# A fused attention and two-stage MoE kernel: a shorter rolled loop for other expert pairs, and one step for each piece of the router

## The chip, the cores and the metric

The kernel runs as one program on one core of a Trainium2 chip. The time is the device time in microseconds (us) of one execution. The profile is of one further execution of the same program. TensorE is called PE, VectorE DVE, ScalarE ACT, GpSimd POOL; SP is the engine that issues most DMAs. PEld is PE's weight load, which overlaps its products.

## The reference, cut to what matters

```python
scores = scale * q @ k.T + bias           # 4 batches, 8 heads, 576 tokens, head size 64
x = (softmax(scores) @ v)                 # -> x [2304, 512], 4 batches of 576 tokens
# first MoE: 8 experts of 512 -> 1024 -> 512, one expert for each token
e_idx = argmax(x @ w_gate);  g = softmax(x @ w_gate)[e_idx];  eom = sigmoid(x @ w_output_gate)
for e in range(8):
    mask = e_idx == e
    out[mask] = g[mask] * eom[mask, e] * (relu(x[mask] @ w1[e]) @ w2[e])
# then a dense gated layer 512 -> 1536 -> 512
return (silu(x @ w_gate) * (x @ w_val)) @ w_out
```

## The kernel before

Attention comes first. The first MoE then works on pairs (batch b, expert e). For each batch the kernel computes the router, finds the first expert that the batch's tokens chose, and runs that expert densely over all 576 tokens, with the gate set to zero for tokens that chose another. Tokens that chose another expert form *other pairs*: one small pair (128 tokens or fewer) is gathered and done by the functions `q_...`; all further pairs go through `loop()`, a loop whose count T is read from the device's list at run time. With T = 0 each engine jumps over the loop's code.

The four dense pairs make 64 steps, numbered n = 16 b + s. At step n PE does `h_step` of step n+1 (12 products, x times a 128-wide slice of w1, into the PSUM tile T) and then `y_step` of step n (12 products with a slice of w2). ACT and DVE turn each h into a high and a low part (tile qz, L544 and L545). After these, step n runs the functions that a table `todo` has for it, in the order in which `at(n, f)` put them there; all engines take their instructions in that order. For batch b = 1, 2, 3 the functions start at n = 16 b - 15 (steps 1, 17, 33):

- `router(b)` has seven pieces: `logits` (PE products lps L370, ACT copies lraw L371), `logits_t` (PE transposes L379, DVE sums L382), `shift` and `gates` (small DVE operations), `gates_2` (DVE L400 to L405, the gates ex), `spread` (PE transposes the gates into gps L412 and counts tokens L415; ACT copies them out L418 to L420; SP stores the gates, L421) and `first` (eight small DVE operations L425 to L432: flags and e0i, the batch's first expert).
- `m_load(b, gi)`: SP reads e0i and loads that expert's weights (L486, L487), the first two parts at step n+7 and n+8; `m_conv` splits slice f into a high and a low half at step n+9+f (ACT and DVE, L503 and L505).
- At step 40 batch 3's `first` is followed by `ranks` of the pair list (PE transposes the flags, L447).

Batch 0's router is done before, by `moe_early`. After step 63 come `q_h` and `q_y` for the small pair (L657 to L672), with `loop()` before the last two slices, then `q_old` (loads xl, L705) and `q_out` (L681 to L700), and after that the dense gated layer (L1179 to L1201), whose weights are narrowed on DVE while its first chunk runs.

Of the kernel before, what the change touches and what calls it, by code (L numbers as in the profile page):

```python
# [9 lines left out]
F32 = mybir.dt.float32  # L10
# [4 lines left out]
ALU = mybir.AluOpType  # L15
# [6 lines left out]
NP = H // 2  # L22
# [11 lines left out]
VL = (7, 12, 13, 14)  # L34
LG = (1, 5, 5, 7, 8, 10, 10)
N0, PRE, FL, LEAD = 6, 3, 0, 0
QN = (43, 46, 44, 46, 49, 54, 56)
EL, EC = ((47, 51, 53), (50, 51, 51, 52, 55, 55))
QT, SX = (44, 2)
# [68 lines left out]
def body(tc, qt, kt, va, vb, ws, moe_w_gate, moe_w_output_gate, moe_w1, moe_w2, w_gate, w_val, w_out, ctab, cst, cst2, out):  # L108
    nc = tc.nc
    with ExitStack() as ctx:  # L110
# [4 lines left out]
        vw = att.enter_context(tc.tile_pool(name="vw", bufs=1))  # L115
# [34 lines left out]
        for r in range(4):  # L150
            o = slice(32 * r, 32 * r + 32)
# [7 lines left out]
        vt = {}  # L159
# [101 lines left out]
        def t_tile():  # L261
            return pO.tile([128, 512], F32, tag="T", bufs=2, name="T")
# [81 lines left out]
        hbuf = {}  # L344
# [135 lines left out]
        def load_w(e, gi, tag="vt"):  # L480

            n = min(3, 8 - 3 * gi)
            t = vw.tile([128, 3072], F32, tag=tag, bufs=1 if tag == "rv" else 2, name="raww")
            a = t[:, 0:512 * n].rearrange("p (k f) -> p k f", k=4)
            c = t[:, 1536:1536 + 512 * n].rearrange("p (f d) -> p f d", f=n)
            nc.sync.dma_start(a, moe_w1[bass.ds(e, 1), :, 384 * gi:384 * gi + 128 * n].rearrange("o (k p) f -> p (o k) f", p=128))  # L486
            nc.sync.dma_start(c, moe_w2[bass.ds(e, 1), 384 * gi:384 * gi + 128 * n].rearrange("o (f p) d -> p (o f) d", p=128))  # L487
            return [(a[:, :, 128 * i:128 * i + 128], c[:, i]) for i in range(n)]
# [3 lines left out]
        def conv_w(raw, f, later=None):  # L492

            a, c = raw
            if f < 4:
                ta = ap.tile([128, 2, 4, 128], F32R, tag="ph", bufs=4, name="w1hl")
                tb = ap.tile([128, 2, 4, 128], F32R, tag="bias", bufs=4, name="w2hl")
            else:
                t = ap.tile([128, 2, 2, 4, 128], F32R, tag=("pt0", "pt1")[f // 6], bufs=2, name="whl")
                ta, tb = t[:, 0], t[:, 1]  # L500
            cc = c.rearrange("p (d m) -> p d m", m=128)
            for x, y in ((a, ta), (cc, tb)):
                nc.scalar.activation(y[:, 0], x, AF.Copy)  # L503
                if later is None:
                    nc.vector.tensor_tensor(y[:, 1], x, y[:, 0].bitcast(F32), ALU.subtract)  # L505
                else:
                    later.append(lambda x=x, y=y: nc.vector.tensor_tensor(y[:, 1], x, y[:, 0].bitcast(F32), ALU.subtract))
            return ta, tb
# [26 lines left out]
        def h_step(ws, xs, s, nq=4, ps=None):  # L535

            o = slice(288 * (s // 8), 288 * (s // 8) + 288)
            ps = (t_tile() if ps is None else ps)[:, 0:288]
            wa = ws[s % 8][0]
            for k in range(4):  # L540
                for i, (x, y) in enumerate(((0, 0), (0, 1), (1, 0))):
                    nc.tensor.matmul(ps, wa[:, x, k], xs[k][y][:, o], start=k == 0 and i == 0, stop=k == 3 and i == 2)  # L542
            t = qhl[s % nq // 2, s % 2]
            nc.scalar.activation(t[:, 0:288], ps, AF.Relu)  # L544
            nc.vector.scalar_tensor_tensor(t[:, 288:576], ps, 0.0, t[:, 0:288].bitcast(F32), ALU.max, ALU.subtract)  # L545

        def y_step(ws, s, nq=4):
            f = s % 8
            if f == 0:
                hbuf["y"] = [pS.tile([128, 2, 512], F32, tag="S", name="y") for _ in range(2)]  # L550
            t = qhl[s % nq // 2, s % 2]
            wb = ws[f][1]
            for d in range(4):
                for i, (x, y) in enumerate(((0, 0), (0, 288), (1, 0))):
                    nc.tensor.matmul(hbuf["y"][d // 2][:, d % 2, 0:288], wb[:, x, d], t[:, y:y + 288],
                                     start=f == 0 and i == 0, stop=f == 7 and i == 2)

        def y_out(gb, s):

            if s < 8:  # L560
                hbuf["out"] = vw.tile([128, 3072], F32, tag="rv", bufs=1, name="yo")[:, 0:NP * S].rearrange("p (d n) -> p d n", d=NP)
            o = slice(288 * (s // 8), 288 * (s // 8) + 288)
            for d in range(4):
                nc.vector.tensor_tensor(hbuf["out"][:, d, o], hbuf["y"][d // 2][:, d % 2, 0:288], gb[:, o], ALU.mult)
# [48 lines left out]
        def q_tok(c):  # L613
            def f():
                n = 64 if c == 4 else 128
                ps = pO.tile([128, 512], F32, tag="pv", bufs=2, name="qps")
                for p in range(NP):
                    nc.tensor.transpose(ps[0:n, 128 * p:128 * p + 128], xq["x"][p][:, 128 * c:128 * c + n], ident)
                nc.scalar.activation(xq["tok"][0:n, c], ps[0:n], AF.Copy)
            return f  # L620
# [115 lines left out]
        def m_conv(b, f, later=None):  # L736
            mu[b]["ws"][f] = conv_w(mu[b]["raw"][f], f, later)
# [87 lines left out]
        for cnt in range(nb + LA):  # L825
            z_iter()
            n = -(-len(extra) // (nb + LA - cnt))
# [13 lines left out]
        for n, (ui, c) in enumerate(steps):  # L841
            p, b = units[ui]
# [22 lines left out]
            old = prev.pop(0) if len(prev) == 2 else None  # L865
# [11 lines left out]
            for hh in range(1 if c == 4 else 2):  # L877
                e = E[:, S * hh:S * hh + S]
# [88 lines left out]
        def at(n, *fs):  # L967
            todo.setdefault(n, []).extend(fs)
        at(QN[0], q_meta)
        at(QT, lambda: xq.update(T=nc.values_load(lst[0:1, 64:65], min_val=0, max_val=28)))  # L970
        at(QR, lambda: xq.update(rot=[nc.values_load(lst[0:1, 67 + j:68 + j], engines=[ENG.SP], min_val=0, max_val=1) for j in range(2)]))
        at(QX, lambda: xq.update(x0=pers.tile([128, NTOK], F32, tag="xT3", name="x0")))
        at(QX, x_first)
        at(QN[1], q_load)
        at(QN[2], q_keep)
        at(QN[3], q_rank)
        for c in range(5):
            at(QN[4] + c, q_tok(c))
        at(QN[5], q_gather)
        at(QN[6], q_selt)  # L980
# [24 lines left out]
        for b in range(1, B):  # L1005
            n = 16 * b - 15
            for i, f in enumerate(mu[b]["sp"]):
                at(n + i // 2, f)
            for i, f in enumerate(router(b)):
                at(n + 4 + i // 2, f)  # L1010
            for gi in range(3):
                at(n + (7, 8, 11)[gi], lambda b=b, gi=gi: m_load(b, gi))
            for f in range(8):
                at(n + 9 + f, lambda b=b, f=f: m_conv(b, f))
            at(16 * b, lambda b=b: m_gate(b))
# [10 lines left out]
        a, z = prev  # L1026
# [13 lines left out]
        for n in range(16 * B):  # L1040
            b, s = divmod(n, 16)
# [15 lines left out]
        def loop():  # L1057

            with tc.For_i(0, xq["T"], 1) as it:
                e = nc.values_load(lst[0:1, bass.ds(it, 1)], engines=[ENG.SP], min_val=0, max_val=7)  # L1060
                bb = nc.values_load(lst[0:1, bass.ds(it + 32, 1)], engines=[ENG.SP], min_val=0, max_val=3)
                gb = ap.tile([128, S], F32, tag="bias5", bufs=1, name="gb")
                nc.sync.dma_start(gb, gscr[bass.ds(bb * 8 + e, 1)].to_broadcast([128, S]))
                old, xr = (ap.tile([128, 18, 256], F16, tag="pt0", bufs=2, name=n).rearrange("p a b -> p (a b)").bitcast(F32).rearrange("p (d n) -> p d n", d=NP) for n in ("old", "xr"))
                for p in range(NP):
                    nc.sync.dma_start(xr[:, p], x1[p, :, bass.ds(bb, 1)].rearrange("p o n -> p (o n)"))
                    nc.sync.dma_start(old[:, p], x2[p, :, bass.ds(bb, 1)].rearrange("p o n -> p (o n)"))
                xs = {}
                for f in split_x(lambda p, b: xr[:, p], 0, 1, xs):
                    f()  # L1070
                for s0 in (0, 8):
                    raw = load_w(e, 0) + load_w(e, 1)
                    ws = {}
                    for s in range(8):
                        if s == 3:
                            raw += load_w(e, 2)
                        ws[s] = conv_w(raw[s], s % 4)
                        h_step(ws, xs, s0 + s, 2)
                        y_step(ws, s0 + s, 2)
                    y_out(gb, s0 + s)  # L1080
                for d in range(NP):
                    nc.vector.tensor_tensor(old[:, d], old[:, d], hbuf["out"][:, d], ALU.add)
                    nc.sync.dma_start(x2[d, :, bass.ds(bb, 1)].rearrange("p o n -> p (o n)"), old[:, d])
                x_first()

# [18 lines left out]
        with ExitStack() as c2:  # L1104
# [4 lines left out]
            xr, xs, rw = {}, {}, {}  # L1109
# [174 lines left out]
```

## Time and profile before

| | |
|---|---|
| time, median of 3 runs | 1062.58 us (1062.15 to 1063.36) |
| profiled execution: its time, its span | 1061.21 us, 1059.0 us |
| granted TensorE clock, mean of the span | 0.984 |
| busy share of the span: PE, PEld, DVE, ACT, POOL | 95%, 76%, 55%, 43%, 11% |

The span runs from the first to the last instruction; 2.2 us of the profiled time lie outside it. Stretches below are us from the span's start. Attention ends at about 330, the MoE steps fill 332 to 577, the small pair 577 to 601, and the gated layer the rest.

### The profile page before, as it was taken

How to read it: one execution, taken by the hardware profiler on the slowest of the kernel's cores; microseconds unless marked ns; L12 is line 12 of the kernel's file. 1: busy time of each engine (PE TensorE's matmuls, PEld its weight loads, DVE VectorE, ACT ScalarE, POOL GpSimd, SP SyncE). 2: the span in 40 equal slices, each digit the busy share in tenths (PEclk: the TensorE clock that was granted, in tenths of full speed). 3: DMA queues.
4: the chain of work that ended last, by engine and by line, in shares of the span. 5: the costliest groups of instructions: out<-in, count | busy, mean ns of one | idle time of the engine just before them, and what ended most of it. 6: DMA issues, size and time to landing. Idle time of an engine off the chain costs nothing. (4 is left out here: it accounts for less than half of the span.)

```text
span 1059.0 us, 18936 instructions
## 1 busy us (share of the span) xinstructions
PE 1008.8 (95%) x7525; PEld 802.9 (76%) x7525; DVE 577.9 (55%) x1321; ACT 457.5 (43%) x1027; POOL 117.1 (11%) x117
## 2 busy tenths in 40 slices
PE   6969999999999899999999799999999999999998
PEld 2337666666667799998999577778888888888897
DVE  8966777676776544454656399972223222322322
ACT  6766777777766333332435354541112111311221
POOL 2662342233210000000000000000000000000000
PEclk9998999999999999999999899999999999999999
DMA  5783333342014041733734455522001000200010
GB/s 189 208 264 114 93 98 101 104 138 92 15 31 128 17 160 56 275 120 128 239 121 145 160 170 177 164 68 70 1 1 49 32 1 1 60 1 1 11 29 20
DMA packets 67756, 101.92 MB, mean 96 GB/s; under 512 B 9136, under 2 KB 37936, under 8 KB 67664
## 3 DMA queue, kind: packets, MB, share of 16 engines
q1 hardware_dynamic: 67504, 100.41, 29.9%
q8 instruction: 61, 1.00, 0.4%
q14 instruction: 31, 0.25, 0.1%
q10 hardware_dynamic: 160, 0.26, 0.1%
HBM read 74.63 MB, written 26.03 MB: 95 GB/s over the span
## 5 line engine op out<-in xcount | busy, mean ns | idle before, releaser
L1179 PE MATMUL v<-x,w 128*128 128x512 f32 (+1 forms) x720 | 161.1, 371 | 4.1 <-DVE w L933 3.8
L1179 PE MATMUL g<-x,w 128*128 128x512 f32 (+1 forms) x720 | 158.5, 369 | 1.1 <-DVE xl L693 0.9
L1179 PEld LDWEIGHTS v<-x,w 128*128 128x128 f32 x720 | 124.9, 189 | 32.3 <-DVE w L933 7.5
L1179 PEld LDWEIGHTS g<-x,w 128*128 128x128 f32 x720 | 126.6, 188 | 25.9 <-ACT x L1134 1.3
L1201 PE MATMUL o<-w,uh 128*128 128x512 f32 x432 | 133.3, 390 | 0.0
L1182 DVE TENSOR_TENSOR t<-g,t 128x512 f32<-128x512 f32 (+1 forms) x60 | 38.2, 637 | 168.1 <-ACT t L1181 168.1
L259 ACT ACTIVATE E<-E,st 128x576 f32<-128x576 f32 x144 | 110.6, 774 | 6.3 <-DVE st L254 6.0
L273 PEld LDWEIGHTS T<-ident,E 64*128 64x128 f32 x1312 | 65.4, 140 | 55.5 <-ACT pt L278 27.4
L254 DVE CUSTOM_DVE_ANT_0 E<-S,bias 128x576 f32<-128x576 f32 x128 | 92.0, 755 | 17.5 <-PE S L250 9.0
L335 PE MATMUL pv<-pt,rawv 128*64 128x256 f32 (+1 forms) x640 | 99.3, 423 | 0.0
L1181 ACT ACTIVATE t<-g 128x512 f32<-128x512 f32 (+1 forms) x60 | 33.2, 553 | 151.8 <-PE g L1179 151.8
L1186 ACT ACTIVATE uh<-t 128x512 fp32r<-128x512 f32 (+1 forms) x60 | 35.4, 589 | 146.2 <-DVE t L1183 146.2
L273 PE MATMUL T<-ident,E 64*128 64x64 f32 x1312 | 92.0, 237 | 6.2 <-ACT rb L323 3.6
L1201 PEld LDWEIGHTS o<-w,uh 128*128 128x128 f32 x432 | 80.3, 188 | 16.1
L280 DVE COPY pt<-T 128x256 f32<-128x256 f32 x160 | 59.6, 414 | 54.3 <-PE T L273 54.2
L1201 PE MATMUL o<-w,ul 128*128 128x512 f32 x216 | 84.0, 389 | 0.0
L250 PE MATMUL S<-kh,qz 64*128 64x288 f32 (+1 forms) x576 | 77.6, 320 | 5.2 <-DVE st L254 4.6
L278 ACT ACTIVATE pt<-T 128x320 f32<-128x320 f32 (+1 forms) x160 | 56.0, 391 | 54.3 <-PE T L273 50.7
L545 DVE SCALAR_TENSOR_TENSOR qz<-T,qz 128x288 fp32r<-128x288 f32 x63 | 28.8, 457 | 86.1 <-ACT qz L544 86.1
L544 ACT ACTIVATE qz<-T 128x288 fp32r<-128x288 f32 x63 | 25.9, 411 | 108.0 <-PE T L542 108.0
L1183 DVE TENSOR_TENSOR t<-v,t 128x512 f32<-128x512 f32 (+1 forms) x60 | 38.3, 638 | 54.9 <-PE v L1179 53.2
L250 PEld LDWEIGHTS S<-kh,qz 64*128 64x128 f32 (+1 forms) x576 | 54.8, 192 | 8.0 <-DVE st L254 5.9
(242 smaller groups left out, 1658.2 us busy)
## 6 DMA issues: line engine op xcount, KB each, us to landing
raww<-in_moe_w_dram SPq DMA_DIRECT2D x16, 768.0 KB, 6.1
bscr<-ob SPq DMA_DIRECT2D x36, 288.0 KB, 3.5
bias<-bscr SPq DMA_DIRECT2D x16, 576.0 KB, 5.0
rw<-in_w_gate_dram SPq DMA_DIRECT2D x12, 512.0 KB, 3.6
rw<-in_w_val_dram SPq DMA_DIRECT2D x12, 512.0 KB, 3.5
rw<-in_w_out_dram SPq DMA_DIRECT2D x12, 512.0 KB, 3.8
rawq<-in_qt_dram SPq DMA_DIRECT2D x16, 320.0 KB, 3.5
rawk<-in_kt_dram SPq DMA_DIRECT2D x16, 288.0 KB, 2.8
```

The costliest lines, as they stand in the source:

```text
L250: nc.tensor.matmul(t[:, f, 0:288], x[k, a], y[k, o], start=i == 0, stop=i == 2)
L254: nc.vector.tensor_tensor_reduce(out=E.rearrange("p (a b) -> p a b", a=2), in0=ps[:, :, 0:288], in1=bt[p, hh, c].rearrange("p (a b) -> p a ...
L259: nc.scalar.activation(E, E, AF.Exp, bias=st[:, 2 * c + hh:2 * c + hh + 1], scale=-1.0, accum_out=st[:, 10 + 2 * c + hh:11 + 2 * c + hh])
L273: nc.tensor.transpose(t[r][:, 64 * j:64 * j + 64], E[k, o:o + 128], ident[k, k])
L278: nc.scalar.activation(o, x, AF.Copy)
L280: nc.vector.tensor_copy(o, x)
L335: nc.tensor.matmul(st["ps"][64 * hh:64 * hh + 64, 0:w], vt[p][:, hh, b, c, :], pts[p, b][f][:, c + (5 * hh if c < 4 else 0), :], start=c = ...
L1179: nc.tensor.matmul(t, a[:, 128 * k:128 * k + 128], x, start=k == 0 and n == 0, stop=k == 3 and n == 2)
L1182: nc.vector.tensor_tensor(t, ps[0], t, ALU.mult)
L1183: nc.vector.tensor_tensor(t, ps[1], t, ALU.mult)
L1186: nc.scalar.activation(uh, t, AF.Copy)
L1201: nc.tensor.matmul(ops[j][m], u[:, o], w, start=f == 0 and n == 0, stop=f == NF - 1 and n == 2)
```

## The change

The body of `loop()` held 16 slices of code (two halves of the tokens, eight weight slices each); it now holds one slice with both halves and runs it in an inner loop over eight weight slices, adding each slice's result to `old`. `y_step` gets a flag for a sum of one slice. The seven pieces of the later batches' routers get the offsets RT = 3, 4, 5, 5, 6, 7, 7 in place of 4, 4, 5, 5, 6, 6, 7: `logits` comes one step earlier and `spread` one step later.

```diff
--- before.py
+++ after.py
@@ -34,6 +34,7 @@
 VL = (7, 12, 13, 14)
 LG = (1, 5, 5, 7, 8, 10, 10)
 N0, PRE, FL, LEAD = 6, 3, 0, 0
+RT = (3, 4, 5, 5, 6, 7, 7)
 QN = (43, 46, 44, 46, 49, 54, 56)
 EL, EC = ((47, 51, 53), (50, 51, 51, 52, 55, 55))
 QT, SX = (44, 2)
@@ -544,7 +545,7 @@
             nc.scalar.activation(t[:, 0:288], ps, AF.Relu)
             nc.vector.scalar_tensor_tensor(t[:, 288:576], ps, 0.0, t[:, 0:288].bitcast(F32), ALU.max, ALU.subtract)
 
-        def y_step(ws, s, nq=4):
+        def y_step(ws, s, nq=4, one=False):
             f = s % 8
             if f == 0:
                 hbuf["y"] = [pS.tile([128, 2, 512], F32, tag="S", name="y") for _ in range(2)]
@@ -553,7 +554,7 @@
             for d in range(4):
                 for i, (x, y) in enumerate(((0, 0), (0, 288), (1, 0))):
                     nc.tensor.matmul(hbuf["y"][d // 2][:, d % 2, 0:288], wb[:, x, d], t[:, y:y + 288],
-                                     start=f == 0 and i == 0, stop=f == 7 and i == 2)
+                                     start=f == 0 and i == 0, stop=(one or f == 7) and i == 2)
 
         def y_out(gb, s):
 
@@ -1006,8 +1007,8 @@
             n = 16 * b - 15
             for i, f in enumerate(mu[b]["sp"]):
                 at(n + i // 2, f)
-            for i, f in enumerate(router(b)):
-                at(n + 4 + i // 2, f)
+            for i, f in zip(RT, router(b)):
+                at(n + i, f)
             for gi in range(3):
                 at(n + (7, 8, 11)[gi], lambda b=b, gi=gi: m_load(b, gi))
             for f in range(8):
@@ -1068,18 +1069,19 @@
                 xs = {}
                 for f in split_x(lambda p, b: xr[:, p], 0, 1, xs):
                     f()
-                for s0 in (0, 8):
-                    raw = load_w(e, 0) + load_w(e, 1)
-                    ws = {}
-                    for s in range(8):
-                        if s == 3:
-                            raw += load_w(e, 2)
-                        ws[s] = conv_w(raw[s], s % 4)
-                        h_step(ws, xs, s0 + s, 2)
-                        y_step(ws, s0 + s, 2)
-                    y_out(gb, s0 + s)
+                with tc.For_i(0, 1024, 128) as fo:
+                    t = vw.tile([128, 3072], F32, tag="vt", bufs=2, name="raww")
+                    a, c = t[:, 0:512].rearrange("p (k f) -> p k f", k=4), t[:, 512:1024]
+                    nc.sync.dma_start(a, moe_w1[bass.ds(e, 1), :, bass.ds(fo, 128)].rearrange("o (k p) f -> p (o k) f", p=128))
+                    nc.sync.dma_start(c, moe_w2[bass.ds(e, 1), bass.ds(fo, 128)].rearrange("o p d -> p (o d)"))
+                    ws = {0: conv_w((a, c), 0)}
+                    for s in (0, 8):
+                        h_step(ws, xs, s, 2)
+                        y_step(ws, s, 2, True)
+                        y_out(gb, s)
+                    for d in range(NP):
+                        nc.vector.tensor_tensor(old[:, d], old[:, d], hbuf["out"][:, d], ALU.add)
                 for d in range(NP):
-                    nc.vector.tensor_tensor(old[:, d], old[:, d], hbuf["out"][:, d], ALU.add)
                     nc.sync.dma_start(x2[d, :, bass.ds(bb, 1)].rearrange("p o n -> p (o n)"), old[:, d])
                 x_first()
 
```

On PE, around the end of step 7 (batch 1's `spread`; h_step is L542 before and L543 now, y_step L555 and L556), the program before reads:

```order
L555 MATMUL y<-qz_116,whl 128x288 [waits Activation_49]
L555 MATMUL y<-qz_116,whl 128x288 [waits DVE_49]
L555 MATMUL y<-qz_116,whl 128x288 x10
L412 MATMUL gps<-ident,ex 8x128 [waits DVE_49,PE_49,Activation_49]
L412 MATMUL gps<-ident,ex 8x128 x3
L412 MATMUL gps<-ident,ex 8x64 [waits PE_49]
L415 MATMUL gps<-oh,cst_sb 1x8 x5
L542 MATMUL T<-xh,w1hl 128x288
```

And now, at the end of step 8:

```order
L556 MATMUL y<-qz_116,whl 128x288 x10
L543 MATMUL T<-xh,w1hl 128x288
L543 MATMUL T<-qz_113,w1hl 128x288
...
L556 MATMUL y<-qz_115,w2hl 128x288 [waits DVE_49]
L556 MATMUL y<-qz_115,w2hl 128x288 x5
L413 MATMUL gps<-ident,ex 8x128 [waits DVE_49,PE_49]
L413 MATMUL gps<-ident,ex 8x128 x3
L413 MATMUL gps<-ident,ex 8x64 [waits PE_49]
L416 MATMUL gps<-oh,cst_sb 1x8 x5
L543 MATMUL T<-xh,w1hl 128x288
```

The transposes gps now stand behind one more h_step and y_step. On DVE nothing changes its place between `gates_2` and `first`; `first` gets a wait for ACT that it did not need before.

On PE at step 40 (batch 3) the program before has gps and the flags' transposes rps a step apart:

```order
L415 MATMUL gps<-oh,cst_sb 1x8 x5
L542 MATMUL T<-xh,w1hl 128x288
...
L555 MATMUL y<-qz_115,w2hl 128x288 [waits Activation_49]
L555 MATMUL y<-qz_115,w2hl 128x288 x11
L447 MATMUL rps<-ident,flags 32x1 [waits DVE_49,Activation_49]
L447 MATMUL rps<-ident,flags 32x1 [waits DVE_49]
L449 MATMUL rps<-rl,cst_sb 32x1 [waits DVE_49]
L542 MATMUL T<-xh,w1hl 128x288
```

and now:

```order
L413 MATMUL gps<-ident,ex 8x128 [waits DVE_49,PE_49]
L413 MATMUL gps<-ident,ex 8x128 x3
L413 MATMUL gps<-ident,ex 8x64 [waits PE_49]
L416 MATMUL gps<-oh,cst_sb 1x8 x5
L448 MATMUL rps<-ident,flags 32x1 [waits DVE_49,Activation_49]
L448 MATMUL rps<-ident,flags 32x1 [waits DVE_49]
L450 MATMUL rps<-rl,cst_sb 32x1 [waits DVE_49]
L543 MATMUL T<-xh,w1hl 128x288
```

The two now follow each other with nothing between them.

On PE at the loop, the program before had a branch, 384 products (16 times 24) and the exit; now there are two nested heads:

```order
L673 MATMUL qy<-whl,qz_115 128x512 x3
L1060 COMPARE_AND_BRANCH
L1060 UNCONDITIONAL_BRANCH x2
L1282 BRANCH_PREFETCH_HINT
L1072 COMPARE_AND_BRANCH
L1072 UNCONDITIONAL_BRANCH x2
L1282 BRANCH_PREFETCH_HINT
L543 MATMUL T<-xh,w1hl 128x288
...
L556 MATMUL y<-qz_115,w2hl 128x288 x12
L1072 REGISTER_ALU
L1072 COMPARE_AND_BRANCH
L1072 UNCONDITIONAL_BRANCH
```

Between them stand 48 products (2 times 24), each with its weight load, where 384 stood.

## Rows read from the trace of the kernel before

**Rows 1.** Waits of PE between 300 and 602: who waited, us, times, longest
```profile
PE gps L412 <- DVE ex L405: 6.4, 3, 2.1
PE qy L672 <- DMA xl<-x: 5.2, 1, 5.2
...
PE T L542 <- ACT rb L323: 1.2, 1, 1.2
```

**Rows 2.** Timeline of PE, batch 1: start, us, line, tile, count, idle before
```profile
367.39 0.74 PE L412 MATMUL gps<-ident,ex 128*8 128x128 f32 x5 [2.14 <-DVE ex L405]
...
368.46 0.42 PE L542 MATMUL T<-xh,w1hl 128*128 128x288 f32 x1
...
374.87 1.75 PE L555 MATMUL y<-qz,w2hl 128*128 128x288 f32 x12
...
378.06 1.75 PE L555 MATMUL y<-qz,w2hl 128*128 128x288 f32 x12
```

**Rows 3.** Stretches: length, busy (instructions) of each engine, granted TensorE clock, DMA
```profile
368.72:372.13 3.41, 3.41 (x16) 3.41 (x16) 0.12 (x1) 0.53 (x3) 0.00 (x0) 0.50 0.03 5
...
332.35:336.50 4.15, 4.15 (x28) 3.49 (x29) 2.06 (x5) 1.89 (x5) 0.00 (x0) 1.00 0.00 0
...
592.18:600.80 8.62, 7.41 (x22) 5.73 (x22) 3.07 (x5) 2.92 (x7) 1.07 (x1) 0.50 0.35 129
```

**Rows 4.** Timelines of DVE and ACT, batch 1's last router pieces
```profile
367.05 0.20 DVE L405 TENSOR_TENSOR ex<-ex 128x40 f32<-128x40 f32 x1
...
368.69 0.15 ACT L420 ACTIVATE cn<-gps 1x8 f32<-1x8 f32 x1
...
372.38 0.15 DVE L425 SCALAR_TENSOR_TENSOR cn<-cn,cst_sb 1x8 f32<-1x8 f32 x1
...
373.41 0.14 DVE L432 CAST e0i<-cn 1x1 int32<-1x1 f32 x1
```

**Rows 5.** Timelines of ACT, DVE and PE, first weight slices of batches 1 and 2
```profile
381.97 0.63 ACT L503 ACTIVATE w2hl<-raww 128x512 fp32r<-128x512 f32 x1 [1.38 <-DMA raww<-in_moe_w_dram]
...
383.25 0.45 DVE L545 SCALAR_TENSOR_TENSOR qz<-T,qz 128x288 fp32r<-128x288 f32 x1
...
384.43 1.75 PE L555 MATMUL y<-qz,whl 128*128 128x288 f32 x12
...
440.54 0.45 DVE L545 SCALAR_TENSOR_TENSOR qz<-T,qz 128x288 fp32r<-128x288 f32 x1
...
442.48 1.75 PE L555 MATMUL y<-qz,whl 128*128 128x288 f32 x12
```

**Rows 6.** Timeline of DVE, batch 3's flags
```profile
488.49 0.14 DVE L425 SCALAR_TENSOR_TENSOR cn<-cn,cst_sb 1x8 f32<-1x8 f32 x1
...
489.27 0.15 DVE L430 COPY flags<-cn 1x8 f32<-1x8 f32 x1
```

**Rows 7.** Line 1059 (the loop): branches of two sequencers, ns min/median/max, first and last start
```profile
L1059 PEldq COMPARE_BRANCH  x3: 101/197/3898, 584.4 to 591.9; - x3
L1059 ACTq COMPARE_BRANCH  x3: 38/38/53, 587.0 to 588.1; - x3
```

**Rows 8.** Timeline of all engines from the loop's jump to the gated layer
```profile
587.26 0.29 DVE L664 SCALAR_TENSOR_TENSOR qz<-qs,qz 128x128 fp32r<-128x128 f32 x1 [0.38 <-ACTq L1059]
588.08 2.95 SPq L705 DMA_DIRECT2D xl<-x  x4
...
592.19 2.93 PE L672 MATMUL qy<-whl,qz 128*128 128x512 f32 x6 [5.25 <-DMA xl<-x]
...
600.20 0.75 DVE L693 TENSOR_TENSOR xl<-xl,qo 128x576 f32<-128x576 f32 x1 [1.17 <-PE qo L689]
```

**Rows 9.** DMA between 586.9 and 592.2: queue, packets, MB, share; issues, us to landing
```profile
q8 instruction: 1, 0.02, 1.7%
...
xl<-x SPq DMA_DIRECT2D x4, 288.0 KB, 4.8
```

**Rows 10.** The stretch after the small pair, columns as in rows 3
```profile
600.00:700.00 100.00, 95.19 (x399) 73.34 (x398) 92.54 (x156) 51.35 (x87) 1.14 (x1) 1.00 0.57 177
```

## The prediction

> **What bounds the kernel now.** PE is busy 95% of the span, so the first view to read is the list of PE's own waits. Between 300 and 602, where the change lies, two entries stand out [rows 1]: gps waits three times for the last gate operation on DVE (6.4 us together, so 2.1 each), and the product qy after the loop's jump waits 5.2. The next entry is only 1.2. The second view is PE's timeline around such a wait: in batch 1 the transposes gps begin at 367.39 after 2.14 of nothing, hence the product before them ended at 365.25 [rows 2]. The third view is the clock by stretches. It fell to 0.50, the 1.2 GHz level, from 368.72 to 372.13, right behind that wait, and stood at 0.50 again from 592.18 to 600.80, behind the loop's jump; behind the wait of 1.2 us it stayed at 1.00 (2.4 GHz) [rows 1, 3]. So a wait here costs twice: once while PE stands, and once in the slower products behind it.
>
> **What one router wait costs.** A step, h_step and y_step, takes 3.19 us at full clock (374.87 to 378.06) [rows 2]. From the end of the counts at 368.46 to 374.87 PE ran one step and one h_step, 6.41 us. At full clock that is one and a half steps, 4.78. The slow clock took 1.63 and the wait 2.14: 3.77 us. Batches 2 and 3 repeat it (the count of three in [rows 1]).
>
> **`spread` a step later.** The gates are finished at 367.25 (L405 at 367.05 plus 0.20) [rows 4]. PE now runs another step first, so gps begins at 365.25 + 3.19 = 368.44, 1.2 us after its inputs. The wait goes, and nothing else that PE executes is added. I take the clock to stay up too, because what is left is 1.07 us of small products without a wait, nearer to the 1.2 us wait that left the clock at 1.00 than to the 2.14 that did not. If it falls all the same, 1.63 for each batch is not won.
>
> **`logits` a step earlier.** Its products and copies are the same ones. No entry of [rows 1] over 1.2 belongs to lps, and x is complete then, so I count nothing.
>
> **`first` in the same step as `spread`.** DVE now stands at `first` until ACT has copied the counts. From gps's start to the end of the count copy L420 it takes 1.45 (367.39 to 368.84), and `first` itself 1.17 (372.38 to 373.55) [rows 2, 4]. Queued behind `first` on DVE is only the next qz; h_step needs 1.6 us before that, so `first` ends about when qz can begin. e0i is then ready at 368.44 + 1.45 + 1.17 = 371.1, 2.4 us earlier than 373.55 in absolute time, while PE is 3.77 ahead. So the weights, which SP requests behind e0i, come 1.4 us later as PE sees them. In batch 1 the second weight half lands at 381.97, ACT and then DVE are held there, qz is ready at 383.25 + 0.45 = 383.70, and the y_step that needs it begins at 384.43: 0.7 us of cover [rows 5]. New: qz at 381.3, y_step wanted at 380.66: a stall of 0.6. In batch 2 the cover is 442.48 - 440.99 = 1.5, enough. SP's store of the gates moves behind the x1 stores of batch 0; the gates are read only steps later, so this costs nothing. Batch 1 gives 3.77 - 0.64 = 3.1, batch 2 gives 3.8.
>
> **Batch 3.** There `ranks` follows in the same step, and its transposes need the flags that `first` writes. From gps's start the flags take 1.45 plus 0.93 (488.49 to 489.42) [rows 6] plus about 0.1 for two hand-overs: 2.5. PE is free after 1.07 (367.39 to 368.46) [rows 2] and then stands 1.4. The wait shrinks by 0.7 and moves. The poor stretch, from gps to the next h_step, is 1.07 + 1.4 + some 0.6 for `ranks` = 3.1 us, close to the 3.2 of before (365.25 to 368.46), so I take the clock to fall here as before. Batch 3 gives 0.7; with the clock up it would give 2.3.
>
> **The loop's jump.** Nothing of the loop's body ran: T was zero, and qy follows the jump at once [rows 8]. PE's sequencer spent 3.898 us in one branch at this line; ACT's longest took 0.053 [rows 7]. In the same 5.3 us one packet of 0.02 MB of instructions came on queue q8 [rows 9]. On PE the jump went over 384 products, each with a weight load, so 768 instructions; ACT's went over some 80. Now it is 48 products, 96 instructions and some 30 of control. I take PE's branch to cost what ACT's costs: the wait of 5.25 becomes 5.25 - 3.90 + 0.05 = 1.40. A floor stands under that: the exit needs DVE's last operation, 587.55 [rows 8].
>
> The Trainium skill (Runtime: NRT & Kernel Launch, Instruction fetch mechanics) says that a taken branch out of the two fetched blocks of 256 instructions stalls for a fetch; by that rule 768 misses and 126 hits, and the trace agrees with the first half by its 3.898 us. The same section gives PE a store of 2048 instructions; by that figure the old jump would have hit already and the loop term would be zero, a total of 1055, but the 3.898 us and the packet speak against it.
>
> What follows the jump is the small pair's end. It ran at 0.50 [rows 3]. With the wait at 1.40, nearer to the 1.2 that left the clock up, I take full clock: then PE's 7.4 us there nearly halve, and the next limit is the fourth xl load, issued last in the four that end at 591.03 (one takes a quarter at least, so about 590.7) and landing 4.8 later, at 595.5 [rows 8, 9]. The last addition L693, now at 600.20, needs it: 4.7 us won at most. At half clock it is 3.85. I take 4.7. All that follows waits for L693 or for PE behind it, and the stage from 600 on has DVE at 92.5 of 100 us [rows 10], with its weights requested by SP behind xl's stores, so it starts earlier as a whole.
>
> **Sum.** 3.1 + 3.8 + 0.7 + 4.7 = 12.3 us from the profiled 1061.21, which gives 1048.9. The profiled execution was 1.4 below the median of 1062.58; taken from the median it is **1050.3**, and I say 1050.
>
> **Rivals.** (a) *The jump still fetches*, because the target lies beyond what PE holds. For it: PE's page limits are not in the trace. Against it: ACT's and DVE's jumps over shorter code. Then 12.3 - 4.7 = 7.6: 1055. (b) *The clock falls without a wait*, at gps in batches 1 and 2: 3.3 less, 1053.6; the three falls seen all had the wait of 2.1 in front. (c) *The router wait comes back elsewhere*, at y_step for late weights, by as much as it was: only the loop's 4.7 stays, 1057.9. Against it: the covers worked out from [rows 5]. (d) *Slower*: `first` gets stuck. If DVE reaches it two steps later than I say, e0i and the weights are 6.4 us late, and each batch's y_step stalls 5 us and more. From 4.9 us of extra stall in each batch on, the whole gain and 2.1 us more are eaten: 1065. What is queued on DVE in that step (one qz of 0.45) does not reach that. (e) *Nothing moves*: T's branch is not what PE waited for, and the router waits are replaced one for one: 1062.
>
> **Chances.** My forecast, with batch 3's clock either way, 0.70; (a) 0.10; (b) 0.09; (c) 0.04; (d) 0.03; (e) 0.04. A change under 0.2%, 2.1 us, could hardly be told from none in this kernel's measurement. Faster by more than that is the forecast with (a), (b) and (c), 0.93; within it (e), 0.04; slower (d), 0.03. The best case is 3.8 + 3.8 + 2.3 + 4.7 = 14.6, so 1048, with some 1.5 for the spread of runs 1046.5. The upper end takes in (a) and (b) one at a time: 1056.
>
> **What the next profile should show.** The entry of gps waiting for ex gone from the waits, gps without idle time in front in batches 1 and 2; the clock at 1.00 behind them; in batch 3 a wait of about 1.4 at the flags' transposes; PE's longest branch at the loop below 0.2 us, and about 1.4 idle before qy; a wait of about 0.6 at a y_step some four steps behind batch 1's gps. The prediction is wrong if PE's branch still takes microseconds, if ACT's wait for the weights grows by more than 2 us, or if the stage after 601 is not earlier by the sum.

## The result and the profile after

The changed kernel takes 1045.68 us (median of 4 runs, 1043.15 to 1047.86); the kernel before, on the same chip, took 1062.97 (1062.15 to 1063.44). The ratio is 0.9839, with a 95% interval of 0.9818 to 0.9859. It is faster, by 17.3 us where 12.3 were forecast, and the time lies 0.8 us below the low end of the range. The profiled execution took 1044.97 us, span 1043.2: 16.2 less than the one of before.

First the list of PE's waits, from 300 to 602 as in [rows 1].

```profile
PE g L1181 <- ACT x L1136: 1.9, 1, 1.9
PE qy L673 <- issue: 1.7, 1, 1.7
PE rps L448 <- DVE cn L432: 1.3, 1, 1.3
PE T L543 <- ACT rb L324: 1.2, 1, 1.2
```

The entry of gps with its three waits is gone, qy waits 1.7 in place of 5.2, and two entries are new: rps in batch 3, which was forecast, and a longer one of g, the first product of the gated layer, which was not: PE is there sooner than the x that it needs.

PE's timeline around batch 1's gps (compare [rows 2]); the first row is the y_step ahead of those in [rows 2].

```profile
363.07 1.74 PE L556 MATMUL y<-qz,whl 128*128 128x288 f32 x12
...
366.25 1.75 PE L556 MATMUL y<-qz,w2hl 128*128 128x288 f32 x12
367.84 0.74 PE L413 MATMUL gps<-ident,ex 128*8 128x128 f32 x5
...
370.63 1.75 PE L556 MATMUL y<-qz,w2hl 128*128 128x288 f32 x12
...
380.19 1.75 PE L556 MATMUL y<-qz,whl 128*128 128x288 f32 x12
```

gps begins with no idle time in front. The last row is the y_step that was forecast to stall for its weights. DVE's and ACT's timelines show why it did not: e0i is ready at 370.36 + 0.14 = 370.50, the second weight half is there at 378.41, qz is ready at 379.69 + 0.45 = 380.14, and PE wants it at 380.19.

```profile
370.36 0.14 DVE L433 CAST e0i<-cn 1x1 int32<-1x1 f32 x1
...
379.69 0.45 DVE L546 SCALAR_TENSOR_TENSOR qz<-T,qz 128x288 fp32r<-128x288 f32 x1
```

```profile
378.41 0.63 ACT L504 ACTIVATE w2hl<-raww 128x512 fp32r<-128x512 f32 x1 [1.65 <-DMA raww<-in_moe_w_dram]
```

The granted clock by stretches (columns as in [rows 3]): behind batch 1's gps, around batch 3's rps, and behind the loop's jump.

```profile
366.25:372.00 5.75, 5.75 (x52) 5.29 (x51) 2.46 (x13) 1.58 (x5) 0.11 (x1) 1.00 0.03 6
478.30:482.20 3.90, 3.61 (x17) 3.60 (x18) 0.64 (x4) 0.13 (x1) 0.13 (x1) 0.56 0.31 54
577.00:586.00 9.00, 4.77 (x23) 3.48 (x23) 3.80 (x7) 4.26 (x10) 1.41 (x1) 1.00 0.62 200
```

It stays at 1.00 in the first and the last, and falls in batch 3 alone. There rps waits 1.34 for the flags, as worked out; the y_steps around it stand for the size of batch 3's term.

```profile
470.85 1.75 PE L556 MATMUL y<-qz,whl 128*128 128x288 f32 x12
...
478.11 0.18 PE L448 MATMUL rps<-ident,flags 1*32 1x1 f32 x2 [1.34 <-DVE cn L432]
...
485.45 1.74 PE L556 MATMUL y<-qz,w2hl 128*128 128x288 f32 x12
```

Now the loop: the branches at its line, as in [rows 7], and the timeline of all engines behind it, as in [rows 8].

```profile
L1060 PEldq COMPARE_BRANCH  x3: 97/187/310, 574.5 to 578.4; - x3
L1060 ACTq COMPARE_BRANCH  x3: 37/38/53, 577.0 to 578.1; - x3
```

```profile
578.47 2.41 SPq L706 DMA_DIRECT2D xl<-x  x4
...
578.69 1.66 PE L673 MATMUL qy<-whl,qz 128*128 128x512 f32 x6 [1.72 <-issue]
...
584.88 0.75 DVE L694 TENSOR_TENSOR xl<-xl,qo 128x576 f32<-128x576 f32 x1 [0.72 <-DMA xl<-x]
...
585.78 3.31 PE L1181 MATMUL g<-x,w 128*128 128x512 f32 x12 [1.86 <-ACT x L1136]
```

PE's longest branch went from 3898 to 310 ns and no longer takes the longest share of the exit. The six products behind it take 1.66 in place of 2.93. L694 now waits for xl and no longer for PE, so the load is the next limit, as forecast.

**A ledger.** Three rows of PE's timeline cut the span: the first y_step, the last one, and the first product g of the gated layer. Before, they start at 334.82, 575.01 and 601.10:

```profile
334.82 1.88 PE L555 MATMUL y<-qz,w2hl 128*128 128x288 f32 x12
...
575.01 1.80 PE L555 MATMUL y<-qz,whl 128*128 128x288 f32 x12
...
601.10 0.47 PE L1179 MATMUL g<-x,w 128*128 128x512 f32 x1 [0.94 <-DVE xl L693]
```

After, at 335.24 and 565.06, and g at 585.78 as shown above:

```profile
335.24 1.85 PE L556 MATMUL y<-qz,w2hl 128*128 128x288 f32 x12
...
565.06 1.80 PE L556 MATMUL y<-qz,whl 128*128 128x288 f32 x12
```

| stretch | before | after | won | forecast |
|---|---|---|---|---|
| to the first y_step | 334.82 | 335.24 | -0.42 | 0 |
| the 64 steps (routers) | 240.19 | 229.82 | 10.37 | 7.6 |
| last y_step to g (loop) | 26.09 | 20.72 | 5.37 | 4.7 |
| from g on | 457.9 | 457.4 | 0.5 | 0 |
| outside the span | 2.2 | 1.8 | 0.4 | 0 |

The two middle cuts are given for every experiment below as well. They say more than the medians on terms of 1 to 2 us, since the runs of one kernel lay 1.3 to 11.2 us apart.

**Where the routers' extra came from.** The y_step ahead of `logits` and the second one behind it show it. Before:

```profile
351.26 1.75 PE L555 MATMUL y<-qz,whl 128*128 128x288 f32 x12
...
360.32 1.75 PE L555 MATMUL y<-qz,whl 128*128 128x288 f32 x12
```

After:

```profile
351.65 1.75 PE L556 MATMUL y<-qz,whl 128*128 128x288 f32 x12
...
359.85 1.78 PE L556 MATMUL y<-qz,whl 128*128 128x288 f32 x12
```

9.06 became 8.20: `logits` a step earlier won 0.86 in batch 1, and by the same rows of the later batches 0.32 (8.51 to 8.19) and 0.33 (8.52 to 8.19). Two waits make this up.

The first is the transposes' wait for ACT's copies, in all three batches. It shows as no idle time in the rows of products. In the rows of weight loads (PEld), which the prediction had not read, the transposes' loads wait twice in batch 1, and the list of PEld's waits shows six such waits, two for each batch:

```profile
357.86 0.20 PEld L379 LDWEIGHTS lps<-ident,lraw 128*128 128x128 f32 x2 [0.58 <-ACT lraw L371]
358.35 0.28 PEld L379 LDWEIGHTS lps<-ident,lraw 128*128 128x128 f32 x3 [0.28 <-ACT lraw L371]
```

```profile
PEld lps L379 <- ACT lraw L371: 2.6, 6, 0.6
```

After, none:

```profile
357.59 0.57 PEld L380 LDWEIGHTS lps<-ident,lraw 128*128 128x128 f32 x5
```

That the loads' idle time of batch 1, 0.58 + 0.28 = 0.86, is the number that batch 1 won is chance: batches 2 and 3 had the same 0.86 and won 0.32 and 0.33. From the first transpose to the next h_step PE took 0.79 (357.86 to 358.65) and takes 0.46 (357.72 to 358.18), so a batch wins about 0.33 here.

The second wait is in batch 1 alone. The h_step ahead of `logits` waited for DVE's half of a split weight slice, 0.20 in the row of products and 0.43 in that of weight loads:

```profile
353.51 0.54 PE L542 MATMUL T<-xh,whl 128*128 128x288 f32 x2 [0.20 <-DVE whl L505]
```

That step took 3.67 from y_step to y_step (351.26 to 354.93), where batch 2's took 3.17 without such a wait: 0.50. Now the products of `logits` stand in front of this h_step, and the wait is gone: 4.48 (351.65 to 356.13) as in batch 2. 0.50 + 0.33 is nearly all of the 0.86.

### The profile page after: what moved, and what is told of

It reads as the page before. It is cut to its first block, busy times and chain, and to the rows that moved or that the text cites. A ratio compares the mean times of both kernels' runs of the same rounds, so it can differ in the third digit from the quotient of the medians.

```text
span 1043.2 us, 18947 instructions
## 1 busy us (share of the span) xinstructions
PE 1000.8 (96%) x7525; PEld 797.0 (76%) x7525; DVE 577.5 (55%) x1321; ACT 456.8 (44%) x1027; POOL 117.1 (11%) x117
```

## Experiments

All were run against the kernel before on the same chip: 1062.65 us (17 runs, 1059.73 to 1065.15) for the first four, 1062.16 (11 runs, 1059.51 to 1064.47) for the next four, 1062.53 (9 runs, 1060.63 to 1064.96) for the last two. "Steps" and "loop" are the cuts of the ledger, in us.

| kernel | median us | ratio, 95% | steps | loop | PE's longest branch us |
|---|---|---|---|---|---|
| e1 routers only | 1051.95 | 0.9905 (0.9886 to 0.9925) | 228.52 | 26.14 | 3.881 |
| e2 loop only | 1057.1 | 0.9955 (0.9939 to 0.9972) | 240.28 | 20.66 | 0.310 |
| e3 `logits` only | 1060.12 | 0.9976 (0.9964 to 0.9988) | 237.07 | 26.95 | 4.782 |
| e4 `spread` only | 1052.37 | 0.9915 (0.9896 to 0.9934) | 230.35 | 24.45 | 3.741 |
| e5 four slices of code | 1046.64 | 0.9857 (0.983 to 0.9884) | 230.20 | 25.77 | 3.510 |
| e6 no loop | 1044.55 | 0.9838 (0.9821 to 0.9856) | 230.30 | 17.83 | none |
| e7 batch 3 a step earlier | 1043.69 | 0.9833 (0.9816 to 0.9851) | 227.30 | 21.17 | 0.187 |
| e8 twice the old body | 1052.04 | 0.9905 (0.9885 to 0.9925) | 228.82 | 24.28 | 3.501 |
| e9 two slices of code | 1045.24 | 0.9835 (0.9816 to 0.9853) | 229.92 | 20.17 | 0.310 |
| e10 = e5 again, one run | 1049.32 | - | 230.51 | 24.33 | 3.621 |

### The two halves: e1_rt and e2_loop

e1_rt is the changed kernel with the old body of `loop()`; e2_loop is the changed kernel with the old offsets:

```diff
-            for i, f in zip(RT, router(b)):
-                at(n + i, f)
+            for i, f in enumerate(router(b)):
+                at(n + 4 + i // 2, f)
```

Expected of e1_rt:

> The router offsets alone; the loop's body stays 384 products long. If the two parts add up as the changed kernel's trace reads (batch 1 4.7, batch 2 4.2, batch 3 1.5, loop 5.4), this is 10.4 us faster than before, 1052.6, with PE's longest branch at the loop near 3.9 us and the clock at 0.50 behind it. By the terms of the prediction it would be 7.6 faster, 1055.4. If most of the gain came from the loop, about 1058.

Expected of e2_loop:

> The short loop body alone; the router pieces stay where they were. Parts that add up: 5.4 us faster than before, 1057.6, three waits of 2.1 us at gps and three falls of the clock as before, PE's longest branch at the loop under 0.4 us. If the jump over less code saves only the branch and not the slow clock behind it: 3.9 faster, 1059.1.

e1 measured 1051.95, 10.7 below before; e2 1057.1, 5.5 below. Their sum is 16.2, and the whole change won 17.3. So the parts add, and neither needs the other. In e1's profile the branch and the wait of qy are those of before; in e2's gps waits as before.

Waits of PE in e2_loop:

```profile
PE gps L413 <- DVE ex L406: 6.4, 3, 2.1
```

Timeline of PE in e1_rt, behind the loop:

```profile
579.77 2.93 PE L673 MATMUL qy<-whl,qz 128*128 128x512 f32 x6 [5.30 <-DMA xl<-x]
```

The timeline names xl as the releaser of qy, but qy does not wait for xl: in e2 qy begins at 588.98, 0.23 us after SP began to issue the same four loads (588.75).

e1 shows one thing more. Batch 3's rps waits 1.34 as in the changed kernel, but the clock stays up:

```profile
477.03 0.18 PE L448 MATMUL rps<-ident,flags 1*32 1x1 f32 x2 [1.34 <-DVE cn L432]
```

```profile
475.50:479.50 4.00, 2.37 (x23) 2.18 (x21) 1.68 (x12) 0.49 (x3) 0.13 (x1) 1.00 0.03 7
```

From the y_step ahead of rps to the second one behind it e1 takes 9.93 us (472.95 to 482.88), the changed kernel 11.41 (474.04 to 485.45). The same routers, the same wait, and 1.48 us between the two levels of the clock.

### The routers' two moves apart: e3_logits and e4_spread

Both with the old loop body. e3_logits moves `logits` alone, e4_spread `spread` alone:

```diff
-RT = (3, 4, 5, 5, 6, 7, 7)
+RT = (3, 4, 5, 5, 6, 6, 7)   # e3_logits
+RT = (4, 4, 5, 5, 6, 7, 7)   # e4_spread
```

Expected of e3_logits:

> Of the router offsets only the first: logits one step earlier, spread where it was, long loop body. Theory: the transposes' weight loads waited for ACT's copies although PE's product rows show no gap; 0.86 + 0.32 + 0.33 = 1.5 us faster than before, 1061.5. The prediction's step (logits costs and gives nothing): 1063.0. Both: gps still waits three times for 2.1.

Expected of e4_spread:

> Of the router offsets only spread one step later, logits where it was, long loop body. Theory: 10.4 less the 1.5 of logits, 8.9 us faster than before, 1054.1; no wait at gps in batches 1 and 2, clock up behind them, a wait of 1.3 at batch 3's flags with the clock falling. If logits gives nothing: 10.4 faster, 1052.6.

e3 is faster by 2.5 us (1.3 to 3.8 by its interval), so `logits` alone does win; the prediction's step, that it costs nothing and gives nothing, falls. Its steps are 3.1 us shorter than before's. 1.5 of that is `logits`, in the same places as in the changed kernel; the rest is the clock. The wait in front of batch 1's gps is 2.15, as in [rows 2], but no fall follows it:

```profile
363.49 1.75 PE L556 MATMUL y<-qz,whl 128*128 128x288 f32 x12
367.38 0.74 PE L413 MATMUL gps<-ident,ex 128*8 128x128 f32 x5 [2.15 <-DVE ex L406]
...
373.33 0.95 PE L556 MATMUL y<-qz,w2hl 128*128 128x288 f32 x6
```

```profile
366.20:372.00 5.80, 4.62 (x41) 4.23 (x42) 2.03 (x13) 1.17 (x4) 0.00 (x0) 1.00 0.02 3
```

363.49 to 373.33 is 9.84 us where before took 363.51 to 374.87, 11.36: 1.52 for the clock (1.63 was worked out), and the rest of what the change won there, 2.3, is the wait.

e4 measured 1052.37, and by the medians `logits` on top of it (e1) gives only 0.4. By the steps it gives 230.35 - 228.52 = 1.8. The medians cannot tell 0.4 from 1.5 here: e4's own runs lie 3.0 us apart, and its median alone would fit the rival's 1052.6. The rows of the trace settle it. Around `logits` e4 takes 9.01, 8.51 and 8.51 us in the three batches, nearly as before, and e1 8.22, 8.19 and 8.21: 0.79 + 0.32 + 0.30 = 1.4. 0.5 more of the 1.8 is a fall of e4's clock over its first steps (335.4 to 338.8). In e4 batch 1's h_step waits for the split weight slice again (0.20), in e3 it does not, so that wait too belongs to `logits`. The fall at batch 3's flags that was expected of e4 did not come.

### What the jump costs: e8_far2, e5_mid, e10_four and e9_two

All have the new routers. e8_far2 has the old loop body twice in a row, so that the jump passes 768 products on PE in place of 384; e5_mid puts four slices of code into the inner loop (192 products) and e9_two two (96), where the changed kernel has one (48). e10_four is e5_mid's kernel once more, for one profile.

```diff
-                for s0 in (0, 8):
+                for s0 in (0, 8, 0, 8):                  # e8_far2, in the old body
-                with tc.For_i(0, 1024, 128) as fo:
+                with tc.For_i(0, 1024, 512) as fo:       # e5_mid (256 and range(2): e9_two)
+                    for j in range(4):
...
```

Expected of e8_far2:

> The changed router offsets with the old loop body written out twice: 768 products in PE's way in place of 384. Theory (one fetch of the target, whatever the distance): the same as the router offsets alone, about 1052.6, PE's longest branch near 3.9 us. Rival (the branch's time grows with the code that is passed): the branch near 7.8 us, about 1057.

Expected of e5_mid:

> The changed kernel with four weight slices of code in the inner loop's body (two passes) in place of one: 192 products, so 384 instructions, in PE's way. Theory (PE must fetch the code it jumps to when it lies too far ahead): the jump is past what PE holds, the branch takes 3 to 4 us again, the clock falls behind it, 5 us slower than the changed kernel, 1051. Rival (qy waits for the join of the engines and for xl, and the shorter body only changed the semaphores): no change, 1045.7.

Expected of e9_two:

> The short loop body with two weight slices of code in the inner loop (four passes) in place of one: the jump passes 96 products, 192 instructions, on PE. The earlier runs showed a branch of 0.31 us over 48 products and of 3.5 us over 192 in the one profiled execution. Theory (a miss is a fixed price that begins somewhere between 96 and 192 products): branch under 0.5 us, idle before qy 1.7, the time of the changed kernel, 1045.7 within 2. Rival (the price begins below 96 products): branch 3.5 or more, idle 4.9 or more, 1049 to 1051.

Expected of e10_four:

> The kernel with four slices of code in the inner loop (192 products, 384 instructions passed) once more, for the branch in a second profiled execution. Its first profile showed a branch of 3.51 us and a time of 1054.8, but the other runs lay between 1043.6 and 1051.9. If the miss belongs to the code's length, the branch is again 3.5 or more and the idle time before qy near 4.9. If it changes from execution to execution, this profile may show 0.3 and 1.7; and if the time is again several us from the first one with the same branch, the spread comes from elsewhere, from where the clock falls.

The branches of PE's sequencer at the loop's line, in e8_far2:

```profile
L1060 PEldq COMPARE_BRANCH  x3: 101/193/3501, 574.5 to 581.7; - x3
```

In e5_mid:

```profile
L1060 PEldq COMPARE_BRANCH  x3: 101/193/3510, 578.0 to 585.2; - x3
```

In e10_four:

```profile
L1060 PEldq COMPARE_BRANCH  x3: 101/193/3621, 575.1 to 582.3; - x3
```

In e9_two:

```profile
L1060 PEldq COMPARE_BRANCH  x3: 101/187/310, 576.2 to 580.2; - x3
```

768 products cost 3.50, 384 cost 3.74 to 4.78 (e4, e1, e3 and before's 3.90), 192 cost 3.51 and 3.62, 96 and 48 cost 0.31. So the price does not grow with the distance. It is a step: paid in full from somewhere between 96 and 192 products (192 and 384 instructions), and not below. The rival of a price by distance, 7.8 us for e8, falls.

That the branch waits for code shows in the place of the instruction packets, not in their number. A packet of 16 KB comes on q8 near the loop in every profile, also in e6, which has no loop, so the one packet of [rows 9] did not by itself speak for a fetch. In all seven profiles with a long branch such a packet starts 0.7 to 1.0 us after the branch begins and ends inside it (before: 588.12 to 589.54, branch 587.13 to 591.03); e3, with the longest branch, 4.78, has two inside. In the four with a short branch (the changed kernel, e2, e7, e9) the next one starts 0.5 to 1.1 us after the branch has ended (the changed kernel: 578.21, branch 577.16 to 577.47).

The Trainium skill's rule of two fetched blocks of 256 instructions (Runtime: NRT & Kernel Launch, Instruction fetch mechanics) would, by an estimate from these figures, put the step between 256 and 512 instructions, depending on where in its block the branch stands. The runs agree with that and do not measure it closer. The store of 2048 instructions that the same section of the Trainium skill gives PE does not agree with them: 384 instructions already cost 3.5 us.

The times say less than the branches. e8 has the time of the routers alone (1052.04 against 1051.95) and e9 that of the changed kernel, as the theories want. e5's runs went from 1043.62 to 1054.8, so that its median of 1046.64 lies near the changed kernel's and not at the 1051 expected, although both profiles of that code show the miss. In the slowest of them the clock stood at half for the whole stretch behind the jump:

```profile
584.50:598.00 13.50, 11.08 (x30) 8.46 (x31) 5.77 (x9) 5.13 (x9) 1.41 (x1) 0.50 0.51 171
```

In e10, with the same branch, it fell only from 582.1 to 585.5. That fits the difference of these two in the loop, 25.77 against 24.33. Whether the miss is there in e5's fastest runs, near 1044, cannot be said: no profile was taken of one.

### Without the loop, and batch 3 moved: e6_none and e7_b3

e6_none leaves out the loop over further pairs altogether, e7_b3 puts all pieces of batch 3's router one step earlier:

```diff
-            if f == LP:                                  # e6_none
-                loop()
-                at(n + i, f)                             # e7_b3
+                at(n + i - (b == 3), f)
```

Expected of e6_none:

> The changed kernel without the loop over other pairs at all (left out: the further pairs, of which this data has none). What is left of the loop in the changed kernel is the join of all engines, 1.7 us without a product, and xl loads that start behind it. Theory: 2 to 3 us faster than the changed kernel, about 1043, with the last L693 addition no longer waiting for xl. If the join is hidden by the small pair's own waits: under 1 us.

Expected of e7_b3:

> The changed kernel with batch 3's router one step earlier, so that a step lies between its flags and the transposes that need them. Theory: the wait of 1.34 and the fall of the clock behind it go, 1.3 + 1.6 = 2.9 us faster than the changed kernel, 1042.8, and the granted clock is 1.00 from the attention to the end. Rival: the pieces collide with the last step of the half (s = 7) on DVE and wait there: no gain.

e6 is 1.1 us faster than the changed kernel by the medians, not 2.7, and only 0.3 if each is taken against the kernel before of its own set of runs (17.6 against 17.3). As expected, its last L694 no longer waits for xl. Its loop stretch is 2.9 shorter, but in its profile the clock then falls from 587.5 to 590.9, where the changed kernel's stays up, and the stretch from g on is 1.8 longer (459.2 against 457.4). In the five profiles whose clock was down within the first 6 us behind g (e1, e2, e5, e6, e7) that stretch took 458.7 to 459.2, in the other seven 457.4 to 457.9. Whether e6's fall belongs to the edit or to the execution is open.

e7 is 1043.69, 2.0 below the changed kernel (1.2 if each is taken against its own kernel before), and its steps are 2.5 shorter. gps and rps of batch 3 now stand a step apart, and rps follows its y_step with no idle time:

```profile
474.22 1.75 PE L556 MATMUL y<-qz,w2hl 128*128 128x288 f32 x12
475.89 0.20 PE L448 MATMUL rps<-ident,flags 1*32 1x1 f32 x2
```

From the y_step of step 39 to that of step 42 e7 takes 469.85 to 481.71, 11.86 us; the changed kernel took 470.85 to 485.45, 14.60. The wait of 1.34 and the slow clock's 1.48 are 2.82, where the difference is 2.74. The expected clock of 1.00 to the end did not come: it fell from 583.1 to 586.5, behind g, and from g on e7 takes 458.9 where the changed kernel takes 457.4. This is the fastest version by the medians; its interval (0.9816 to 0.9851) and the changed kernel's (0.9818 to 0.9859) overlap, so the order of the two rests on the trace more than on the medians.

## Why the prediction was right in kind and too low in size

The sign, the places and the mechanisms of `spread` and of the jump held. The step that failed is the sum: it took 0.64 off for a stall that did not come, counted `logits` as nothing where it won 1.5, batch 3 as 0.7 where it won 1.2, and the loop as 4.7 where it won 5.4. That is 3.3 us, and with it the low end of the range went wrong:

- **`spread` a step later, batches 1 and 2: right.** 3.77 each was worked out; 363.07 to 370.63 is 7.56 where 363.51 to 374.87 took 11.36, so 3.80 in batch 1. The clock stayed up behind gps, rival (b) did not come.
- **The stall of 0.64 at batch 1's weights: wrong.** No wait took the place of the one removed: qz was ready at 380.14, PE there at 380.19. The way from gps to e0i was as worked out (367.84 to 370.50, 2.66; 368.44 to 371.1). What was off is the load behind it, taken over from before: from e0i to ACT's part of the second weight half it took 8.42 us there (373.55 to 381.97) and takes 7.91 now (370.50 to 378.41). Half a microsecond less was most of the stall of 0.64. Why the load took less stays open, and the cover is thin: in e5 and e8, with the same routers, the same y_step (at 383.34 and 381.27) had its weight loads wait 0.23 and 0.25 for qz, and its step took 3.46 and 3.49 in place of 3.18. So the term lies between 0 and some 0.3.
- **`logits` counted as nothing: wrong, and the largest miss.** 0.86 + 0.32 + 0.33 = 1.5 us. "No entry over 1.2 belongs to lps" was true and no argument. The copies of ACT held the transposes, which cost 0.3 in each batch and stands only in the rows of weight loads, and in batch 1 the moved products fill a wait of another tile (whl), 0.5.
- **Batch 3: 0.7 forecast, 1.2 measured with the clock down** (479.59 to 495.35 was 15.76, 470.85 to 485.45 is 14.60). The wait went from 2.15 to 1.34, the worked-out 1.4. With the clock up, as in e1, it is 2.6 (13.11), where 2.3 was named. That the clock fell, as forecast, was partly luck: the poor stretch that was given as the reason is the same in e1, e4 and e8, which had no fall.
- **The loop: 4.7 forecast, 5.4 measured.** The branch became 0.31, not 0.05, and the wait before qy 1.72, not 1.40; that cost nothing, since the xl load was the limit, as said. From SP's first issue to the last addition it took 6.4 us (578.47 to 584.88), where 7.4 was reckoned: SP issued the four in 2.41 us, not 2.95, and the landing took 4.2 us, not 4.8. 0.3 of this was lost again, since SP began that much later behind the last y_step. The clock stayed up. That what e2 removes is the code's fetch rests on e5, e8, e9 and e10, where the branch follows the amount of code passed as a step, and on the place of the packets.
- **The base.** Nothing moved in the runs of before (1062.97 against 1062.58), so the miss is not there. By the profiled pair the change won 16.2: 10.4 + 5.4 in the terms above, -0.4 ahead of them, and 0.9 from the gated layer on and outside the span, which no experiment explains. The medians' 17.3 is 1.1 more, less than single runs differ.
- **The range.** Its best case already had no stall (3.8 for batch 1) and the clock up in batch 3 (2.3), but `logits` at zero and the loop at 4.7. With the 1.5 and 0.7 that these two won beyond it, its low end would have been 1044.3 in place of 1046.5. A term counted as nothing should have been let be a gain as well.

Rivals (a) and (c) to (e) did not come either; the mechanism of (a) is what e5 and e10 show for a body of 192 products.

## What to carry to other kernels

Code that never runs can be on the path: if a loop is usually skipped, look at the branch's duration on the engine whose code is longest there, and keep its body short; the price is a step, so shortening only helps once it passes the step. A wait of 2 us in front of PE may cost 1.5 more in the clock behind it, so a producer's piece one step earlier or its consumer one step later can be worth nearly twice the wait. Before a move is counted as nothing, compare the starts of the steps around it with those of a step that does not have it. The waits of products alone hide small losses, and the idle time of weight loads overstates them: the transposes' loads waited 2.6 us in three batches, and PE won 1.0 of that.

## What had not been expected of the hardware

- **The same wait did not always bring the same clock.** Of nine waits of 2.1 in front of gps (before, e2, e3), eight were followed by a fall to 1.2 GHz and one, in e3, was not. Of the eight profiles with a wait of 1.34 in front of rps (the changed kernel, e1, e4, e5, e6, e8, e9, e10), five had a fall there and three, e1, e4 and e8, had none. The 1.2 us wait near 333, which left the clock up in [rows 3], was followed by a fall in e3, e4, e6, e8 and e10. So "the wait brings the fall" is a tendency, and a term that rests on the clock has two values, 1.5 us apart.
- **Falls like these go with the spread of runs.** The first y_step began between 334.02 and 338.37 in the twelve profiles, with the same attention code ahead of it. The five whose clock stayed up between 300 and that point (before, the changed kernel, e1, e2, e7) began it between 334.02 and 335.24; three with one fall there (e3, e8, e10) between 335.11 and 336.29; the four with two such falls or one twice as long (e4, e5, e6, e9) between 336.86 and 338.37. e5, the latest, had one more from 62.1 to 65.5.
- **A jump over 192 products or more cost 3.5 to 4.8 us on PE, and it cost 768 no more than 192** (3.50 against 3.51 and 3.62).
